# First-stage stores issued from GpSimd's queue, sums in a buffer of their own, longer transfer allowances in the planner

## The chip, the cores and the metric

The kernel runs on one core of a Trainium2 chip. The metric is device time in microseconds (us) of one execution. Five engines work side by side, each through its own instructions in a fixed order: TensorE (PE in the profile) multiplies, VectorE (DVE) and ScalarE (ACT) compute on tiles, GpSimd (POOL) and SyncE (SP) here issue transfers (DMAs). An instruction that has to wait holds back everything behind it on its engine, a transfer's issue included.

## The reference

Three steps, 4608 tokens (8 batches of 576), model width 512, inner width 2048:

```python
k_p = k.reshape(B, H, S // 8, 8, D).mean(axis=3)      # keys and values pooled by 8
v_p = v.reshape(B, H, S // 8, 8, D).mean(axis=3)
attn = softmax(q @ k_p.T / sqrt(D))                   # 8 heads of 64
x = (attn @ v_p) as [4608, 512]
x = square(relu(x @ w_in)) @ w_out                    # first feed-forward block
h = x @ w2_in
out = maximum(0.01 * h, h) @ w2_out                   # second feed-forward block
```

The four weight matrices arrive as 64-bit floats, which the kernel reads as pairs of 32-bit words and turns into 32-bit floats itself.

## The kernel before

**Stages.** The program has three stages one after the other. The first (about 0 to 604 us of the trace) computes attention and `h1 = square(relu(x @ w_in))`; the second (`Middle`) multiplies h1 by w_out; the third (`Second`) is the second feed-forward block. Each product is split into high and low parts, so a 512-column product takes three matmuls.

**The first stage.** Tokens go in 9 blocks of 512 (`blk`), inner columns in 16 groups of 128 (`c`). One pair (blk, c) is a *unit*: 12 matmuls of 512 columns into one PSUM bank (line 999), a relu out of the bank into a tile `r` or `st` (line 1010), a square in place (line 1013), and a store of 256 KB to `h1` in HBM (line 1029). The second stage multiplies by a scheme with sums, so for even blocks the sum of two neighbouring units' squares is stored too (addition at line 1035, store at line 1038). Tiles `r`, and `st` for odd units from block 2 on, have three buffers each; a relu waits until the buffer it is to write has been read by everyone, its store included.

**The order.** `START` and the first 16 units (`first_products`, `HAND = 16`) stand in an order written by hand; their stores go to GpSimd's queue. All that follows in the first stage is put in order by a planner: `FirstStage` lists operations with their engine, a cost in us, a rank, what they come after (`after`) and which buffers they take (`gets`) or touch (`uses`), and `Plan.run` always takes the operation that can start first by these figures. The figures only decide the order in which instructions stand on each engine; the chip then runs each engine's list in order, whatever the true durations are. A transfer counts as finished `lag` us after its issue. In the planned part the stores go to SyncE's queue, the same that loads keys, values, queries and words:

```python
def dma(self, fn, rank, kb, n=1, **k):
    return self.op("SP", 0.35 * n, fn, rank, lag=2.2 + kb / 180.0, **k)
```

**Attention's chain.** For each batch, keys and values are loaded (`add_keys`, `add_v`: 1 MB each, a key tail of 128 KB into `raw`, a value remainder of 384 KB in six transfers) and pooled on VectorE (the key tail at line 567). For each tile of 128 tokens, TensorE transposes q (line 681) and computes scores (line 727), ScalarE and VectorE make probabilities, TensorE transposes these (line 807, and line 815 for the last keys), ScalarE copies the high part out of the bank (line 821), VectorE the low part (line 824), and TensorE multiplies with the values (lines 868 to 871). All of these take PSUM banks from one set of four, `ps`.

**Words.** `add_stored` converts 38 half-tiles of the later weights within the first stage: load (line 345), exponent on ScalarE (line 243), bits and terms on VectorE (lines 247 to 264), sums (line 407), stores of 128 to 512 KB.

**Sums.** Before, the sum of an even block is added in place, into the first of the two squares' tiles, and the store of the sum reads that tile. The addition therefore has to wait until the store of that first square has read its tile.

Of the kernel before, what the change touches and what calls it, by code (L numbers as in the profile page):

```python
# [9 lines left out]
F32 = mybir.dt.float32  # L10
# [6 lines left out]
P = 128  # L17
# [26 lines left out]
def attention_relu2_leaky_kernel(  # L44
# [266 lines left out]
    class Weights:  # L311
# [5 lines left out]
        def load(self, n):  # L317
            self.steps[n][0]()
# [10 lines left out]
    class Stored:  # L329
# [10 lines left out]

        def load(self, h, tag="val"):
            w, kind, _, i, n = self.jobs[h]
            t = sb([P, 512, 2], U32, tag)
            for src, to in half_words_of(w, kind, i, n):
                nc.sync.dma_start(out=to(t), in_=src)
            return t[:, :, 0], t[:, :, 1]
# [674 lines left out]
    def store_parts(blk, c, r, queue):  # L1021

        t0 = blk * T
        n = T if blk else T // 2
        late = slice(t0 + T - n, t0 + T)
        s = {}

        def square_out():
            queue.dma_start(out=h1[c // 2, :, c % 2, t0 : t0 + T], in_=r())
            if c % 2 == 0:  # L1030
                evens[blk, c // 2] = r()

        def total():
            s[0] = evens[blk, c // 2][:, T - n :]
            nc.vector.tensor_tensor(out=s[0], in0=s[0], in1=r()[:, T - n :], op=ALU.add)

        def total_out():
            queue.dma_start(out=h1[c // 2, :, 2, late], in_=s[0])

        return [square_out] + ([total, total_out] if c % 2 and not blk % 2 else [])  # L1040
# [129 lines left out]
    class Plan:  # L1170

        SLACK = {"PE": 1.5, "ACT": 0.3, "DVE": 0.3, "SP": 0.3}

        def __init__(self, counts):
            self.ops, self.counts, self.rings, self.n = [], counts, {}, 0

        def op(self, engine, us, fn, rank, after=(), gets=(), uses=(), lag=0.0):
            x = Op(engine, us, fn, rank, lag)  # L1180
            for y in after:
                if y is not None:
                    y.then.append(x)
                    x.waits += 1
            x.gets = list(gets)
            for b in (*gets, *uses):
                b.users.append(x)
            x.order = len(self.ops)
            self.ops.append(x)
            return x  # L1190
# [16 lines left out]
        def run(self):  # L1207
# [3 lines left out]
            while left:  # L1211
# [17 lines left out]
                x.fn()  # L1229
                for y in x.then:  # L1230
                    y.ready = max(y.ready, x.end + x.lag + self.SLACK[y.engine])
                    y.waits -= 1
                    if not y.waits:
                        open_.append(y)
            self.now = now

    class FirstStage:
# [17 lines left out]
        def dma(self, fn, rank, kb, n=1, **k):  # L1255
            return self.op("SP", 0.35 * n, fn, rank, lag=2.2 + kb / 180.0, **k)

# [177 lines left out]
        def add_unit(self, blk, c, n):  # L1435
# [17 lines left out]
            x = self.plan.op("ACT", 0.63, lambda: square(at["r"]), 2, after=[x], uses=[r])  # L1453
            steps = store_parts(blk, c, lambda: at["r"], nc.sync)
            y = self.plan.op("SP", 0.35, steps[0], 0, after=[x], uses=[r], lag=3.0)
            if len(steps) > 1:
                x = self.plan.op("DVE", 0.69 if blk else 0.42, steps[1], self.SUMS,
                                 after=[x, self.even], uses=[r, self.even_r])
                self.plan.op("SP", 0.35, steps[2], 0, after=[x], uses=[self.even_r], lag=3.0)
            self.even, self.even_r = y, r  # L1460

        def add_stored(self, jobs):
            words, before = {}, None
            for h in jobs:
                _, kind, name, i, n = stored.jobs[h]
                val, gl = Buffer(f"wo{h % 2}"), Buffer("gl")
                R = self.STORED
                st = {}

                def run(fn, st=st):  # L1470
                    return lambda: fn(st)

                x = self.dma(run(lambda st, h=h: st.update(zip(("low", "top"), stored.load(h, f"wo{h % 2}")))),
                             R, 512, n=1 + kind, gets=[val], after=[self.units[2, 0]])
                x = self.op("ACT", 0.67, run(lambda st: exponent(st["top"])), R, after=[x], uses=[val])
# [43 lines left out]
        def run(self):  # L1519
# [26 lines left out]
            stored.at = STORED_EARLY  # L1546
            attention += self.last
            self.add_second_stage(attention)
            plan.run()

        def add_second_stage(self, attention):
            plan, last = self.plan, BLOCKS - 1
            opened_ = plan.op("SP", 0.0, middle.open, 0, after=attention)
            for four in (0, 1):
                for p in range(PAIRS):
                    if four:
                        after = [self.units[last, 2 * p + 1]]
                    else:
                        after = attention + [self.units[last - 1, FC - 1]]
                    x = plan.op("SP", 0.35, lambda four=four, p=p: middle.load_weights(four, p), 5,  # L1560
# [7 lines left out]
            for g in range(3):  # L1568
                x = plan.op("SP", 0.7, lambda g=g: middle.load(g), 5,
                            after=[opened_, self.units[last, 5 + g]], lag=5.0)  # L1570
                if g < 2:
                    steps = {}
# [12 lines left out]
    class Middle:  # L1585
# [16 lines left out]
        def open(self):  # L1602
            opened.pop().release()
            pool = tc.alloc_tile_pool(name="ms", bufs=1, side="left", reuse_waits="tile")
            opened.append(pool)
            nc.gpsimd.memset(pool.tile([P, 56], F32, tag="off", name="off"), 0.0)
            POOLS.update({f"m{n}{i}": pool for n in "hl" for i in range(3)})
# [80 lines left out]
        def group(self, g):  # L1688
            t0, n, r, four, p = self.at(g)
            steps = []  # L1690
            for x in range(g + 1, min(g + 5, self.GROUPS)):
                l, e = self.ahead(x)
                if x - l == g:
                    steps.append(lambda x=x: self.load(x))
            for x in range(g + 1, min(g + 3, self.GROUPS)):
                if x - self.ahead(x)[1] == g:
                    steps += self.prepare(x)
# [586 lines left out]
```

## Time and profile before

| | |
|---|---|
| median of three runs | 1687.83 us (1687.49 to 1690.32) |
| the profiled execution, its own time | 1688.77 us |
| its span, first to last instruction | 1687.0 us |
| TensorE busy | 1629.1 us (97% of the span) |
| VectorE busy | 1266.8 us (75%) |
| ScalarE busy | 835.6 us (50%) |
| mean TensorE clock that was granted | 0.992 of full speed |

So 1.77 us of the profiled execution lie outside the span. TensorE is busy nearly all the time; the profile's clock line falls below full speed only where TensorE has just stood. The second and third stages run from about 605 us to the end.

### The profile page before, as it was taken

Reading aid. Unit: us, or ns where it says so; the run is one execution under the profiler, and the core shown is the slowest. Engines: PE = TensorE matmul, PEld = TensorE weight load, DVE = VectorE, ACT = ScalarE, POOL = GpSimd, SP = SyncE. Lnnn points to the kernel's source line nnn. Section 1 sums busy time; section 2 is a strip of 40 time slices with the busy share of each in tenths; the row PEclk is TensorE's granted clock in tenths of the full one; section 3 lists DMA queues with packets and bytes.
Section 4 is the critical chain, followed back from the end, with each engine's and each line's share of the span. In section 5 each row is a group of like instructions: output and inputs, shape, how many; then the busy total and the mean of one; then the engine's idle time right before and its main releaser. Section 6 shows DMA issues by size and latency. Waiting matters only on the chain. (4 is left out here: it accounts for less than half of the span.)

```text
span 1687.0 us, 26627 instructions
## 1 busy us (share of the span) xinstructions
PE 1629.1 (97%) x9560; PEld 1472.9 (87%) x9560; DVE 1266.8 (75%) x2214; ACT 835.6 (50%) x1797; POOL 14.6 (1%) x30
## 2 busy tenths in 40 slices
PE   7897999989999979999999999999999999999998
PEld 6786887778888878888888899999999999999998
DVE  6885589878875488786869978878867876666665
ACT  6665676646765564434434554434444643333332
POOL 0110000000000000000000000000000000000000
PEclk9998999999999999999999999999999999999999
DMA  8726576768567977665758676476548754554443
GB/s 240 255 76 181 152 235 204 216 221 256 178 231 241 311 255 239 205 232 190 244 177 287 232 241 216 159 235 220 183 152 258 263 181 150 159 158 156 151 151 107
DMA packets 282756, 345.78 MB, mean 205 GB/s; under 512 B 55360, under 2 KB 201280, under 8 KB 282624
## 3 DMA queue, kind: packets, MB, share of 16 engines
q1 hardware_dynamic: 280480, 338.57, 62.0%
q0 software_dynamic: 1568, 4.98, 0.8%
q8 instruction: 75, 1.23, 0.3%
q10 hardware_dynamic: 576, 0.52, 0.1%
q14 instruction: 57, 0.47, 0.1%
HBM read 208.74 MB, written 135.27 MB: 204 GB/s over the span
## 5 line engine op out<-in xcount | busy, mean ns | idle before, releaser
L999 PE MATMUL acc<-xh,wi 128*128 128x512 f32 x640 | 224.9, 408 | 4.9 <-ACT r L1010 3.6
L999 PE MATMUL acc<-wo,wi 128*128 128x512 f32 x704 | 191.4, 399 | 8.8 <-ACT r L1010 8.8
L999 PEld LDWEIGHTS acc<-wo,wi 128*128 128x128 f32 x704 | 130.0, 189 | 35.0 <-ACT r L1010 9.6
L999 PEld LDWEIGHTS acc<-xh,wi 128*128 128x128 f32 x640 | 122.9, 192 | 30.7 <-ACT r L1010 4.6
L999 PE MATMUL acc<-xl,wi 128*128 128x512 f32 x320 | 127.1, 397 | 0.1
L2168 PE MATMUL ps<-wi,hh 128*128 128x256 f32 x512 | 93.9, 283 | 0.0
L2168 PE MATMUL acc<-wi,hh 128*128 128x256 f32 x496 | 91.1, 283 | 0.0
L2168 PE MATMUL ps<-wo,hh 128*128 128x256 f32 x496 | 90.9, 283 | 0.0
L1662 ACT CAST mh<-ms 128x512 fp32r<-128x512 f32 (+2 forms) x68 | 52.5, 771 | 76.7 <-DVE ms L1644 76.7
L2168 PE MATMUL acc<-wo,hh 128*128 128x256 f32 x484 | 88.8, 283 | 0.0
L1925 PE MATMUL acc<-fh,wo 128*128 128x384 f32 x384 | 83.0, 338 | 3.1 <-DVE gh L1938 2.0
L1010 ACT ACTIVATE r<-acc 128x512 f32<-128x512 f32 x88 | 53.2, 608 | 62.8 <-PE acc L999 38.5
L749 ACT ACTIVATE s<-ps,m 128x72 f32<-128x72 f32 x240 | 74.1, 334 | 19.3 <-DVE m L737 19.2
L1925 PE MATMUL ps<-fh,wi 128*128 128x384 f32 x384 | 82.3, 336 | 0.2 <-DVE gh L1938 0.2
L1941 ACT ACTIVATE gh<-gh 128x384 f32<-128x384 f32 x48 | 25.3, 527 | 112.3 <-DVE gh L1938 112.3
L2168 PEld LDWEIGHTS ps<-wi,hh 128*128 128x128 f32 x512 | 79.9, 192 | 0.0
L2168 PEld LDWEIGHTS acc<-wi,hh 128*128 128x128 f32 x496 | 77.4, 192 | 0.0
L2168 PEld LDWEIGHTS ps<-wo,hh 128*128 128x128 f32 x496 | 77.4, 192 | 0.0
L1707 PE MATMUL acc<-mh,wi 128*128 128x512 f32 (+1 forms) x256 | 77.2, 367 | 0.1
L1707 PE MATMUL ps<-mh,wi 128*128 128x512 f32 (+1 forms) x256 | 77.1, 367 | 0.0
L2168 PEld LDWEIGHTS acc<-wo,hh 128*128 128x128 f32 x484 | 75.5, 192 | 0.0
L2168 PE MATMUL ps<-wi,hl 128*128 128x256 f32 x256 | 72.4, 283 | 0.0
(350 smaller groups left out, 4365.9 us busy)
## 6 DMA issues: line engine op xcount, KB each, us to landing
h<-r SPq DMA_DIRECT2D x104, 256.0 KB
hf<-r SPq DMA_DIRECT2D x96, 192.0 KB
ml<-h SPq DMA_DIRECT2D x34, 512.0 KB
ml<-h SPq DMA_DIRECT2D x60, 256.0 KB
hr<-hf SPq DMA_DIRECT2D x23, 640.0 KB
xl<-hf SPq DMA_DIRECT2D x23, 640.0 KB
xh<-hf SPq DMA_DIRECT2D x23, 640.0 KB
h<-st SPq DMA_DIRECT2D x56, 256.0 KB
```

The source lines that it names most:

```text
L749: nc.scalar.activation(out=s[:, g, :], in_=at["ps"][:, h * SP : (h + 1) * SP], func=AF.Exp, bias=m[:, g : g + 1], accum_out=l[:, g : g + 1],)
L999: nc.tensor.matmul(acc_of[blk, c], lhsT=(wih, wil)[w][c][:, kc], rhs=xsplit[blk][x][kc], start=(kc, n) == order[0], stop=(kc, n) == order[-1],
L1010: nc.scalar.activation(out=r, in_=ps, func=AF.Relu)
L1662: nc.scalar.copy(hi[:, at], y)
L1707: nc.tensor.matmul(at[s][:, :n], lhsT=w[:, wx, b, s * P : (s + 1) * P], rhs=x[:, a], start=p == 0 and m == 0, stop=p == PAIRS - 1 and m == 2,)
L1925: nc.tensor.matmul(at, lhsT=w[:, FORMS[j], kc], rhs=x[j][:, kc], start=m == 0 and j not in (4, 6), stop=m == 5, skip_group_check=True,)
L1941: nc.scalar.activation(out=out_, in_=x, func=AF.Lrelu)
L2168: nc.tensor.matmul(at[:, s * TR : (s + 1) * TR], lhsT=x[:, a, s * P : (s + 1) * P], rhs=w[:, b], start=p == 0 and s == 0 and m == 0, stop= ...
```

## The change

Five edits, all of which act on the first stage and its end:

1. In the planned part, stores of squares and sums are issued from GpSimd's queue instead of SyncE's (the planner counts 1.0 us for an issue and 4.0 us until the transfer has landed; before 0.35 and 3.0).
2. The sum goes into a buffer of its own (`gh`, for block 0 `wo3`), so the addition no longer writes into a tile that is being stored.
3. The planner counts `5.0 + kb / 90` us for a transfer from SyncE's queue instead of `2.2 + kb / 180`: 6.4 us instead of 2.9 for the key tail of 128 KB, 16.4 instead of 7.9 for 1 MB.
4. Words are loaded two halves to a tile (the halves' loads stand right behind one another, `behind=`), and may start after unit (1, 12) instead of unit (2, 0).
5. At the end of the stage: weights of the second stage whose tiles the words don't use wait for attention only; the parts of group 2 of the second stage are prepared within the plan; a small GpSimd memset goes away.

```diff
         def square_out():
             queue.dma_start(out=h1[c // 2, :, c % 2, t0 : t0 + T], in_=r())
-            if c % 2 == 0:
+            if c % 2 == 0 and blk % 2 == 0:
                 evens[blk, c // 2] = r()
 
         def total():
-            s[0] = evens[blk, c // 2][:, T - n :]
-            nc.vector.tensor_tensor(out=s[0], in0=s[0], in1=r()[:, T - n :], op=ALU.add)
+            s[0] = sb([P, T], F32, "gh" if blk else "wo3")[:, :n]
+            even = evens.pop((blk, c // 2))
+            nc.vector.tensor_tensor(out=s[0], in0=even[:, T - n :], in1=r()[:, T - n :], op=ALU.add)
...
-        SLACK = {"PE": 1.5, "ACT": 0.3, "DVE": 0.3, "SP": 0.3}
+        SLACK = {"PE": 1.5, "ACT": 0.3, "DVE": 0.3, "SP": 0.3, "POOL": 0.3}
...
         def dma(self, fn, rank, kb, n=1, **k):
-            return self.op("SP", 0.35 * n, fn, rank, lag=2.2 + kb / 180.0, **k)
+            return self.op("SP", 0.35 * n, fn, rank, lag=5.0 + kb / 90.0, **k)
...
-            steps = store_parts(blk, c, lambda: at["r"], nc.sync)
-            y = self.plan.op("SP", 0.35, steps[0], 0, after=[x], uses=[r], lag=3.0)
+            steps = store_parts(blk, c, lambda: at["r"], nc.gpsimd)
+            y = self.plan.op("POOL", 1.0, steps[0], 0, after=[x], uses=[r], lag=4.0)
             if len(steps) > 1:
+                total = Buffer("gh" if blk else "wo3")
                 x = self.plan.op("DVE", 0.69 if blk else 0.42, steps[1], self.SUMS,
-                                 after=[x, self.even], uses=[r, self.even_r])
-                self.plan.op("SP", 0.35, steps[2], 0, after=[x], uses=[self.even_r], lag=3.0)
+                                 after=[x, self.even], gets=[total], uses=[r, self.even_r])
+                self.plan.op("POOL", 1.0, steps[2], 0, after=[x], uses=[total], lag=4.0)
...
+                first = x = self.dma(run(load), R, 512, n=1 + kind, gets=[val] if n == 0 else (),
+                             uses=[val], after=[self.units[1, 12]], behind=first if n else None)
...
-                        after = attention + [self.units[last - 1, FC - 1]]
+                        after = both if p in (0, 1, 3) else attention
+                        after = after + [self.units[last - 1, FC - 1]]
...
-                if g < 2:
+                if g < 3:
```

**Where it moves instructions.** First SyncE's list where the planned part begins; `wo` tiles receive keys, values and words, `raw` queries and key tails, and `h` is h1. Before:

```order
L193 DMA wo_1209<-in_v 32x1x512 x6
L1029 DMA h_77<-r 128x512
L183 DMA wo_1243<-in_v 128x4x512
L1029 DMA h_77<-r 128x512 x2
L176 DMA wo_1286<-in_k 128x4x512
L212 DMA raw<-in_q 128x8x64 x2
L163 DMA raw<-in_k 64x512
L1038 DMA h_77<-r 128x256
L1029 DMA h_77<-r 128x512 x2
L176 DMA wo_1384<-in_k 128x4x512
L1038 DMA h_77<-r 128x256
```

The same stretch of SyncE's list in the change:

```order
L193 DMA wo_1239<-in_v 32x1x512 x6
L183 DMA wo_1305<-in_v 128x4x512
L176 DMA wo_1365<-in_k 128x4x512
L212 DMA raw<-in_q 128x8x64 x2
L163 DMA raw<-in_k 64x512
L212 DMA raw<-in_q 64x8x64 x2
L212 DMA raw<-in_q 128x8x64
L183 DMA wo_1600<-in_v 128x4x512
L346 DMA wo_1623<-in_moe_w_out 128x2x256 x4
L346 DMA wo_1642<-in_moe_w_out 128x2x256 x4
```

The stores are gone from it, to GpSimd's list (144 of squares and 40 of sums there now, 16 and 6 before), and two runs of four word loads stand ahead of where they began before.

Next VectorE's list in the part written by hand, at the first sum, with the semaphores that each instruction waits for (`DMASW` counts transfers of GpSimd's queue). Before:

```order
L307 TENSOR_TENSOR wi_470<-wo_464,wi_470 128x1024 [waits Activation_49]
L1035 TENSOR_TENSOR r<-r 128x256 [waits DMASW0_49,Activation_49]
L737 TENSOR_REDUCE m<-acc_531 128x4 [waits PE_49]
L737 TENSOR_REDUCE m<-ps 128x4 [waits PE_49]
L261 TENSOR_SCALAR wi_126<-wo_516 128x1024 [waits DVE_49]
```

And in the change:

```order
L307 TENSOR_TENSOR wi_470<-wo_464,wi_470 128x1024 [waits Activation_49]
L1037 TENSOR_TENSOR wo_526<-r 128x256 [waits Activation_49]
L738 TENSOR_REDUCE m<-acc_532 128x4 [waits PE_49]
L738 TENSOR_REDUCE m<-ps 128x4 [waits PE_49]
L261 TENSOR_SCALAR wi_126<-wo_516 128x1024 [waits DVE_49]
```

The order is the same; the addition no longer waits for a store, and the two score maxima behind it are what ScalarE's exponentials need.

Last TensorE's list where block 1 ends and block 2 begins (from `acc_1733`'s last parts on before, `acc_1671`'s in the change; the units of block 2 read `xh` and `xl`). Before:

```order
L999 MATMUL acc_1733<-wo_821,wi_1099 128x512
L868 MATMUL ps<-pth,v_hi 128x384
L869 MATMUL ps<-pth,v_lo 128x384
L870 MATMUL ps<-ptl,v_hi 128x384
L871 MATMUL ps<-ptr,v_rem 128x384
L999 MATMUL acc_1733<-wo_821,wi_1099 128x512
L999 MATMUL acc_1733<-st,wi_1099 128x512
L999 MATMUL acc_1733<-wo_821,wi_1099 128x512
```

In the change:

```order
L1000 MATMUL acc_1671<-wo_824,wi_1105 128x512
L808 MATMUL ps<-cst,s 128x128 x4
L816 MATMUL ps<-cst,prem_84 96x128 x2
L550 MATMUL ps<-cst,gh 128x128 x4
L556 MATMUL ps<-cst,km 128x64
L869 MATMUL ps<-pth,v_hi 128x384
L870 MATMUL ps<-pth,v_lo 128x384
L871 MATMUL ps<-ptl,v_hi 128x384
L872 MATMUL ps<-ptr,v_rem 128x384
```

The last probability transposes now stand right ahead of the value products that need them, with only the last keys' and two key transposes between, and no part of a unit of block 1 is left to stand among the value products.

## Rows read from the trace of the kernel before

Times are in us unless marked ns.

**Rows 1.** The page: its head, and the first line of busy times.

```profile
span 1687.0 us, 26627 instructions
...
PE 1629.1 (97%) x9560; PEld 1472.9 (87%) x9560; DVE 1266.8 (75%) x2214; ACT 835.6 (50%) x1797; POOL 14.6 (1%) x30
```

**Rows 2.** Windows: length, busy by engine (instructions), then granted clock, DMA share, GB/s.

```profile
45.00:85.00 40.00, 33.71 (x184) 28.33 (x184) 32.84 (x50) 27.16 (x84) 6.07 (x10) 0.96 0.78 248
...
125.00:160.00 35.00, 26.22 (x132) 21.69 (x130) 14.21 (x33) 15.24 (x60) 0.00 (x0) 0.85 0.59 173
160.00:250.00 90.00, 88.70 (x489) 75.27 (x488) 64.93 (x163) 66.16 (x229) 0.00 (x0) 1.00 0.64 193
250.00:262.00 12.00, 8.32 (x38) 6.65 (x37) 9.23 (x22) 4.86 (x21) 0.00 (x0) 0.86 0.51 162
...
298.00:325.00 27.00, 24.40 (x133) 19.51 (x132) 23.66 (x54) 19.41 (x73) 0.00 (x0) 1.00 0.69 207
...
362.00:380.00 18.00, 12.85 (x60) 10.53 (x59) 13.06 (x28) 9.94 (x37) 0.00 (x0) 0.81 0.71 232
380.00:590.00 210.00, 210.00 (x1009) 174.83 (x1007) 147.14 (x322) 130.47 (x324) 0.29 (x2) 1.00 0.75 243
590.00:600.00 10.00, 6.36 (x21) 5.11 (x22) 5.30 (x8) 7.01 (x11) 0.00 (x0) 0.83 0.71 237
...
605.00:625.00 20.00, 15.13 (x112) 13.79 (x113) 17.52 (x34) 8.99 (x18) 0.00 (x0) 1.00 0.83 274
```

**Rows 3.** Timelines near 65 us: start, length, instruction, in brackets idle before and releaser.

```profile
65.47 0.43 DVE L1035 TENSOR_TENSOR r<-r 128x256 f32<-128x256 f32 x1 [2.94 <-DMA h<-r]
...
68.89 0.56 PE L681 MATMUL ps<-cst,raw 128*128 128x128 f32 x2 [3.47 <-ACT s L749]
```

**Rows 4.** Timelines of SyncE's queue, ScalarE and TensorE, 127 to 151 us.

```profile
127.09 4.23 SPq L193 DMA_DIRECT2D wo<-in_v  x6
...
132.32 0.38 SPq L183 DMA_DIRECT2D wo<-in_v  x1
132.81 1.63 SPq L1029 DMA_DIRECT2D h<-r  x2
...
144.14 0.60 ACT L1010 ACTIVATE r<-acc 128x512 f32<-128x512 f32 x1 [4.35 <-DMA h<-r]
...
150.50 0.60 ACT L1010 ACTIVATE r<-acc 128x512 f32<-128x512 f32 x1 [5.76 <-DMA h<-r]
...
144.79 0.80 PE L999 MATMUL acc<-wo,wi 128*128 128x512 f32 x1 [4.07 <-ACT r L1010]
```

**Rows 5.** Source lines 1029 and 1038: GpSimd's issues, and from issue to landing.

```profile
L1038 POOL DMA_DIRECT2D h<-r x6: 542/546/1049, 54.7 to 106.3; - x6
...
DMA to landing us min/median/max: 2.0/3.7/6.6
...
DMA to landing us min/median/max: 2.3/2.5/6.3
```

**Rows 6.** Timelines of SyncE's queue and VectorE: one key tail, issue and use.

```profile
242.51 0.53 SPq L163 DMA_DIRECT2D raw<-in_k  x1
...
252.42 1.00 DVE L567 TENSOR_REDUCE kp<-raw 64x64 f32<-64x512 f32 x1 [5.60 <-DMA raw<-in_k]
```

**Rows 7.** Waits of VectorE, 45 to 625 us: in total, times, longest.

```profile
DVE r L1035 <- DMA h<-r: 20.6, 9, 6.6
...
DVE kp L567 <- DMA raw<-in_k: 10.7, 2, 5.6
```

**Rows 8.** Timelines of VectorE and ScalarE at 365 and 593 us.

```profile
365.01 0.69 DVE L1035 TENSOR_TENSOR r<-r,st 128x512 f32<-128x512 f32 x1 [6.63 <-DMA h<-r]
...
592.99 0.60 ACT L1010 ACTIVATE r<-acc 128x512 f32<-128x512 f32 x1 [5.39 <-DMA h<-r]
```

**Rows 9.** Timeline of TensorE at 189 us; groups by form (count, busy, mean ns), 125 to 600 us.

```profile
189.22 0.49 PE L999 MATMUL acc<-xh,wi 128*128 128x512 f32 x1 [1.21 <-ACT xh L880]
...
L821 ACT CAST pth<-ps 128x512 fp32r<-128x512 f32 x28 | 16.6, 593 | 17.7 <-PE ps L807 17.3
...
L824 DVE TENSOR_TENSOR ptl<-ps,pth 128x512 fp32r<-128x512 f32 x28 | 19.3, 688 | 3.1 <-ACT pth L821 2.7
```

More of the change, by code (lines that the diff above doesn't have):

```diff
@@ L339, in begin, with load @@
             self.at = end
-        def load(self, h, tag="val"):
+        def load(self, h, t=None):
             w, kind, _, i, n = self.jobs[h]
-            t = sb([P, 512, 2], U32, tag)
+            if t is None:
+                t = sb([P, 512, 2], U32, "val")
             for src, to in half_words_of(w, kind, i, n):
@@ L1170, in attention_relu2_leaky_kernel, with op @@
     class Plan:
-        SLACK = {"PE": 1.5, "ACT": 0.3, "DVE": 0.3, "SP": 0.3}
+        SLACK = {"PE": 1.5, "ACT": 0.3, "DVE": 0.3, "SP": 0.3, "POOL": 0.3}
         def __init__(self, counts):
             self.ops, self.counts, self.rings, self.n = [], counts, {}, 0
-        def op(self, engine, us, fn, rank, after=(), gets=(), uses=(), lag=0.0):
+        def op(self, engine, us, fn, rank, after=(), gets=(), uses=(), lag=0.0, behind=None):
             x = Op(engine, us, fn, rank, lag)
@@ L1182, in op @@
                 if y is not None:
-                    y.then.append(x)
+                    y.then.append((x, True))
                     x.waits += 1
+            if behind is not None:
+                behind.then.append((x, False))
+                x.waits += 1
             x.gets = list(gets)
@@ L1229, in run @@
                 x.fn()
-                for y in x.then:
-                    y.ready = max(y.ready, x.end + x.lag + self.SLACK[y.engine])
+                for y, ends in x.then:
+                    if ends:
+                        y.ready = max(y.ready, x.end + x.lag + self.SLACK[y.engine])
                     y.waits -= 1
@@ L1465, in add_stored @@
                 _, kind, name, i, n = stored.jobs[h]
-                val, gl = Buffer(f"wo{h % 2}"), Buffer("gl")
+                if n == 0:
+                    val, tiles = Buffer(f"wo{i % 2}"), {}
+                gl = Buffer("gl")
                 R = self.STORED
@@ L1471, in run, with load @@
                     return lambda: fn(st)
-                x = self.dma(run(lambda st, h=h: st.update(zip(("low", "top"), stored.load(h, f"wo{h % 2}")))),
-                             R, 512, n=1 + kind, gets=[val], after=[self.units[2, 0]])
+                def load(st, h=h, i=i, n=n, tiles=tiles):
+                    if n == 0:
+                        tiles[0] = sb([P, 2, 512, 2], U32, f"wo{i % 2}")
+                    st["low"], st["top"] = stored.load(h, tiles[0][:, n])
+                first = x = self.dma(run(load), R, 512, n=1 + kind, gets=[val] if n == 0 else (),
+                             uses=[val], after=[self.units[1, 12]], behind=first if n else None)
                 x = self.op("ACT", 0.67, run(lambda st: exponent(st["top"])), R, after=[x], uses=[val])
@@ L1546, in run, with add_second_stage @@
             stored.at = STORED_EARLY
-            attention += self.last
-            self.add_second_stage(attention)
+            self.add_second_stage(attention, attention + self.last)
             plan.run()
-        def add_second_stage(self, attention):
+        def add_second_stage(self, attention, both):
             plan, last = self.plan, BLOCKS - 1
@@ L1605, in open @@
             opened.append(pool)
-            nc.gpsimd.memset(pool.tile([P, 56], F32, tag="off", name="off"), 0.0)
             POOLS.update({f"m{n}{i}": pool for n in "hl" for i in range(3)})
@@ L1694, in group @@
                     steps.append(lambda x=x: self.load(x))
-            for x in range(g + 1, min(g + 3, self.GROUPS)):
+            for x in range(max(g + 1, 3), min(g + 3, self.GROUPS)):
                 if x - self.ahead(x)[1] == g:
```

## Prediction

> **What bounds the kernel now.** I read the page's busy line first: TensorE works 1629.1 of 1687.0 us, VectorE three quarters of the time and ScalarE half [rows 1]. So nothing is gained by making another engine faster; time is gained only where TensorE stands, and the two later stages run without a gap worth naming. The windows come next, because they say where it stands: length less TensorE's busy time. That is 6.29 us in 45 to 85, 8.78 in 125 to 160, 1.30 in 160 to 250, 3.68 in 250 to 262, 2.60 in 298 to 325, 5.15 in 362 to 380, nothing in 380 to 590, 3.64 in 590 to 600 and 4.87 in 605 to 625 [rows 2]: 36 us. Five of these stretches also show a granted clock under full speed. One minus the clock, times the length, is 1.6, 5.25, 1.7, 3.4 and 1.7 us, 13.6 together. As TensorE stood for a part of that time, only a part of it was lost; I take half, with nothing and all as bounds.
>
> Then the timelines, for who ends the waits. In the part written by hand the first sum stands 2.94 us for a store, and TensorE then stands 3.47 us behind the exponentials whose maxima are queued behind that sum [rows 3]. At 125 to 160 two stores are issued behind six remainder loads (4.23 us of issuing) and a load of 1 MB; they are issued at 132.81, and the relu that needs the tile starts at 144.14, 11.3 us later, after 4.35 us of standing; another stands 5.76 us, and TensorE stands behind the relu [rows 4]. At 252 the key tail is used 9.9 us after its issue, VectorE having stood 5.60 us [rows 6]; the planner had counted 2.9. At 365 it is a sum again, 6.63 us, and at 593 a relu, 5.39 us [rows 8]. VectorE's waits say the same in total: 20.6 us for stores ahead of sums, 10.7 us for key tails [rows 7]. So every large stall is an engine standing in order at an instruction whose transfer came later than the planner thought.
>
> **The change part by part.** *Stores from GpSimd.* The same stores, issued by hand from GpSimd earlier on, cost 542 ns to issue (1049 at worst) and landed after 2.3 to 3.7 us in the median, 6.6 at worst [rows 5], in a stretch with more traffic (248 GB/s) than the 173 GB/s of 125 to 160, where SyncE's took 11.3 [rows 2, 4]. The planner now counts 1.0 + 4.0 us for them, which covers the median. 184 issues of 0.54 us are 100 us on an engine that is busy 14.6 [rows 1, 5], so issuing costs nothing; its cover is that GpSimd has no other work. If a sum is late, its store holds up the next unit's store and so a tile `r`, of which there are three. Recovered in full, 125 to 160 is worth 8.78 + 2.6 = 11.4 us, 362 to 380 5.15 + 1.7 = 6.9, and 590 to 600 3.64 + 0.85 = 4.5. With three tiles some waits for the unit before must remain, so I take 8.5, 5.0 and 3.5, about three quarters; bounds nothing and all.
>
> The Trainium skill, "DMA: Bandwidth & Descriptors", section "Issuing engines are not separate DMA queues", says that transfers of all issuers run on the same 16 DMA engines and interleave, and that another issuer saves only the issuing. By that the stores would land about as late as before; what it gives is the first rival. The rows on GpSimd's landing times speak against it here.
>
> The Trainium skill, "SBUF — State Buffer", section "🔬 SBUF: two separate sides", warns that VectorE in a two-port mode can keep GpSimd from writing a transfer's descriptors. The longest issue in the trace of before is 1.05 us beside a median of 0.54, so if that happened it was short; by the rule some stores would be issued later, but the sum above doesn't take it in.
>
> *A buffer for the sum.* The 2.94 us of wait in the hand part goes, with its likes, and with it most of 45 to 85: 6.29 + 0.8 = 7.1 at most; part of the idle time there is of other waits, so 5.5. The sums at 365 are in the term above.
>
> *Longer allowances.* The key tail counts 6.4 us now (6.7 with slack), against 9.9 measured [rows 6]. Of the 7 us by which it came late, 3.5 are now planned around. So of 250 to 262 (3.68 + 0.85 = 4.5) I take 2.5, and of 298 to 325 (2.60), where the other long key wait of [rows 7] lies, 2.2, since the stores no longer stand in front of the tail's queue either. Bounds nothing and all.
>
> *Words.* Two halves to a tile make runs of 1 MB, and two runs, 2 MB, can now stand ahead of a key or value load; at 248 GB/s [rows 2] that is 8.5 us. The values are needed many units later, so mostly it costs nothing; what hides it is the units' matmuls planned ahead, and only block 2's attention is just in time. There I charge the moved order: where it turns from block 1 to 2, the last probability transposes stand right ahead of their value products, and the copies between, 593 ns on ScalarE and 688 ns on VectorE (some 0.4 more for the last keys' part, worked out as its share of the columns), have only short transposes beneath, where TensorE idled 1.21 before [rows 9]. Between no loss and 2.5 us, I take 1. For other waits that a new order brings with it I take 3: the lower bound is the 210 us of the same planner without a gap, the upper two new stalls as at 250 to 262, 3.68 + 1.7 each, 11 us.
>
> *The end.* With group 2 prepared within the plan and weights loaded earlier, of 4.87 us in 605 to 625 [rows 2] I take half, 2.4; bounds nothing and all. The memset is one instruction on an idle engine: nothing.
>
> The sum: 5.5 + 8.5 + 2.5 + 2.2 + 5.0 + 3.5 + 2.4 = 29.6, less 4 is 25.6 us. From the profiled execution's own 1688.77 that is 1663.2; the median of the runs is 0.9 lower than that execution, so **1662 us**. All idle time and all clock back without a new cost would be 50 us, 1638; half of the terms with the whole of the costs is 14.8 − 13.5, nearly no gain.
>
> **The rivals.** *The queue doesn't matter.* If the same DMA engines make the stores land as late as before, the relus go on standing; left are 5.5 + 2.5 + 2.2 + 2.4, half of the 5.0 (the sum no longer waits, the relu does), less 4: 11.1 us, **1677**. For it: in 125 to 160 the stores stood behind bulk loads that will still run. Against it: [rows 5]. 0.12.
>
> *New waits eat the gain.* Word runs 8.5 us long ahead of a load that is just in time: two of them late by that much, in full on TensorE, cost 17 us, and with 5 of clock 22, which leaves 4: **1684**, and 1678 to 1690 around it. For it: attention of blocks 2 and later is fed by loads that stand behind words on one queue. Against it: the longer allowances make the planner start what depends on them later. 0.12, of which 0.04 still faster, 0.06 the same and 0.02 slower.
>
> *The sums' buffer becomes the stall, and the kernel slower.* From block 2 on 32 sums go to `gh`, which has two buffers and which the masked keys use too. If each sum has to wait until an earlier store has landed at the worst value seen, 6.6 us [rows 5], against 5.3 counted with slack, VectorE stands 1.3 us each; the maxima behind it are what ScalarE and then TensorE wait for. 32 by 1.3 is 42 us: **1704**. It decides from 25.6 / 32 = 0.8 us of TensorE's time for each sum. For it: in the hand part 2.94 us of one such wait reached TensorE as 3.47 [rows 3]. Against it: two buffers leave a unit pair's time, and later blocks have slack in VectorE. 0.08, of which 0.01 the same.
>
> **How the numbers follow.** The forecast gets 0.68, with a range of its own of 1648 to 1670: the low end is all of the 36 us of idle time and half of the clock's 13.6, less 3 of cost (40 us), the high end four fifths of the terms with 2 us more of costs (18 us). Over all cases 1648 to 1682 leaves out some 0.15: the slower rival, half of the second, a little below. A change of less than 0.2%, 3.4 us, is about what a measurement of this kernel can't tell from none. Faster: 0.68 + 0.12 + 0.04 = 0.84; the same: 0.06 + 0.01 = 0.07; slower: 0.02 + 0.07 = 0.09.
>
> **What would show it.** The step on the queue is right if GpSimd's list has some 190 issues of about 0.54 us, landing in 2 to 7 us, if ScalarE's waits for stores are gone and TensorE is busy through the stretch that answers to 125 to 160. The sum's buffer is right if VectorE's 20.6 us at line 1035 fall to nearly nothing. The allowances are right if the wait at the key tail is half of 10.7 or less. The cost at the turn to block 2 shows as TensorE waiting for ScalarE's or VectorE's copies of probabilities. Wrong would make it: stores from GpSimd landing after 10 us, a wait of VectorE for the sums' stores, or loads of keys and values standing behind words.

## The result, and the profile after

| | before | after |
|---|---|---|
| median of the runs beside each other | 1688.62 us | 1660.01 us (1658.12 to 1662.21, 4 runs) |
| ratio | | 0.983, 95% interval 0.9813 to 0.9847 |
| the profiled execution, its own time | 1688.77 us | 1660.31 us |
| span | 1687.0 us | 1658.5 us |

The change makes the kernel 1.7% faster, 28.6 us by the medians; 1662 was forecast. The page's busy line, against [rows 1]:

```profile
PE 1618.0 (98%) x9560; PEld 1470.8 (89%) x9560; DVE 1264.1 (76%) x2214; ACT 834.4 (50%) x1797; POOL 102.4 (6%) x191
```

TensorE's busy time fell by 11.1 us with the same 9560 matmuls, and its idle time (span less busy) from 57.9 to 40.5 us, by 17.4; together these are the 28.5 us of the span. The windows of the first stage show where it stood less, against [rows 2]; the stretches are moved where the program now gets there earlier. The columns are those of [rows 2].

```profile
45.00:85.00 40.00, 38.45 (x227) 32.67 (x226) 38.41 (x61) 31.05 (x106) 7.64 (x12) 1.00 0.81 263
...
125.00:160.00 35.00, 33.29 (x181) 28.06 (x180) 24.70 (x60) 21.24 (x77) 5.44 (x10) 1.00 0.65 194
...
160.00:200.00 40.00, 34.66 (x179) 28.41 (x178) 32.64 (x80) 26.98 (x105) 3.24 (x6) 0.91 0.74 225
...
240.00:252.00 12.00, 5.05 (x15) 4.20 (x16) 7.54 (x18) 5.68 (x22) 0.00 (x0) 0.60 0.64 185
...
298.00:325.00 27.00, 27.00 (x147) 22.81 (x146) 23.91 (x60) 21.81 (x88) 3.24 (x6) 1.00 0.75 214
...
362.00:380.00 18.00, 17.00 (x94) 13.71 (x93) 17.31 (x43) 13.35 (x56) 3.79 (x7) 1.00 0.80 235
```

Length less TensorE's busy time was 6.29 us at 45 to 85 and is 1.55; 8.78 at 125 to 160, now 1.71, with the clock at 1.00 in place of 0.85; 2.60 at 298 to 325, now nothing; 5.15 at 362 to 380, now 1.00. Two stretches became worse: 160 to 200 idles 5.34 us, and 240 to 252 idles 6.95 at a granted clock of 0.60. In the first, TensorE's longest stand is one of 2.7 us where block 1 turns into block 2, at 172.09: the key transposes (line 550) wait for the masked keys that VectorE writes at line 524. The timelines of SyncE's queue, VectorE and TensorE show the second:

```profile
235.82 1.02 SPq L410 DMA_DIRECT2D w1o<-wo  x1
...
244.16 0.43 DVE L408 TENSOR_TENSOR wo<-gl 128x256 f32<-128x256 f32 x1 [9.40 <-DMA w1o<-wo]
...
246.94 1.12 PE L682 MATMUL ps<-cst,raw 128*128 128x128 f32 x4 [7.92 <-DVE ptl L825]
```

Line 410 stores a part of a converted word from the tile that line 408 writes for the next word. The store was issued 8.3 us before VectorE got on, on the queue on which a run of four word loads had been issued just before (at 225.80), and TensorE stood 7.92 us. The waits over 45 to 625 us (in total, times, longest), against [rows 7], and then GpSimd's stores, against [rows 5]:

```profile
ACT r L1011 <- DMA h<-r: 6.7, 2, 3.9
...
DVE wo L408 <- DMA w1o<-wo: 16.4, 4, 9.4
...
PE ps L550 <- DVE gh L524: 2.7, 1, 2.7
```

The same kernel, the source line that issues the stores:

```profile
L1030 POOL DMA_DIRECT2D h<-r x88: 539/539/829, 47.1 to 585.1; - x88
...
DMA to landing us min/median/max: 2.3/4.2/7.1
```

VectorE's 20.6 us for stores at the sums and 10.7 us at the key tails are gone from its list, ScalarE's waits for stores are 6.7 us where they were 22.7, and GpSimd's stores of squares took 0.54 us each to issue and landed after 2.3 to 7.1 us. These are the signs that the prediction named, but for ScalarE's waits, which it wanted gone. But a kernel can show every sign and owe its time to something else, so the edits were taken apart.

The three stages in us, the first from the span's start, each to the first matmul of the next (in TensorE's timeline), the third to the end of its last matmul, all from the one profiled execution; the last column is the median of each kernel's own runs:

| kernel | first | second | third | median |
|---|---|---|---|---|
| before | 604.2 | 360.1 | 718.2 | 1688.62 |
| after | 584.1 | 351.0 | 718.8 | 1660.01 |
| b_queue | 599.6 | 365.0 | 718.2 | 1692.28 |
| b_sum | 588.4 | 360.4 | 720.5 | 1672.70 |
| b_sum_queue | 593.3 | 360.2 | 717.6 | 1676.74 |
| b_lag | 629.6 | 355.7 | 718.3 | 1711.80 |
| a_queue | 587.7 | 353.5 | 720.0 | 1667.12 |
| a_inplace | 593.8 | 355.3 | 718.8 | 1672.19 |
| a_lag | 594.7 | 351.9 | 718.7 | 1673.16 |
| a_words | 606.4 | 349.0 | 718.0 | 1678.34 |
| a_end | 584.7 | 360.5 | 719.3 | 1669.64 |
| a_words_out | 584.1 | 351.1 | 718.5 | 1663.03 |
| a_store8 | 607.9 | 348.7 | 718.9 | 1681.88 |
| a_store6_32 | 586.3 | 353.5 | 755.2 | 1699.82 |

So 20.1 us of the gain lie in the first stage and 9.1 in the second. TensorE's idle time in the first stage fell from 44.3 to 29.4 us; in the second from 5.5 to 2.7.

### The profile page after: what moved, and what is told of

Same layout as the page of the kernel before. It is cut to its first block, busy times and chain, and to the rows that moved or that the text cites. A ratio compares the mean times of both kernels' runs of the same rounds, so it can differ in the third digit from the quotient of the medians.

```text
span 1658.5 us, 26685 instructions
## 1 busy us (share of the span) xinstructions
PE 1618.0 (98%) x9560; PEld 1470.8 (89%) x9560; DVE 1264.1 (76%) x2214; ACT 834.4 (50%) x1797; POOL 102.4 (6%) x191
## 5 line engine op out<-in xcount | busy, mean ns | idle before, releaser
L1000 PE MATMUL acc<-xh,wi 128*128 128x512 f32 x640 | 221.3, 403 | 0.1
```

Source lines behind the costliest of these rows:

```text
L1000: nc.tensor.matmul(acc_of[blk, c], lhsT=(wih, wil)[w][c][:, kc], rhs=xsplit[blk][x][kc], start=(kc, n) == order[0], stop=(kc, n) == order[-1],
```

## The experiments

Names that begin with b_ are the kernel before with one part of the change (two in b_sum_queue); with a_, the changed kernel without one part, and in the last three with something more. Ratios are to runs of the kernel before on the same chip.

**The stores' queue, with the order on TensorE, VectorE and ScalarE kept.** The same edit in the one kernel and undone in the other:

```diff
-            steps = store_parts(blk, c, lambda: at["r"], nc.sync)     # b_queue
+            steps = store_parts(blk, c, lambda: at["r"], nc.gpsimd)   # undone in a_queue
```

> The kernel before with one edit: the planned part's stores are issued from GpSimd; the planner's figures, and with them the order on TensorE, VectorE and ScalarE, stay as before; sums still in place. If the queue is what made the stores late, the three terms of the prediction for it come back, 8.5 + 5.0 + 3.5 = 17 us (bounds 0 and 22.8): about 1671 us, ScalarE's 22.7 us of waits for stores gone, GpSimd's stores landing in 2 to 7 us. If the same DMA engines make them late whatever the queue: 1688 within 3 us, landings near 10 us. If the order had to change too: half of it, about 1679.

b_queue measured 1.0007 (0.9997 to 1.0016): nothing. Its waits over 45 to 625 us (in total, times, longest):

```profile
DVE r L1035 <- DMA h<-r: 28.7, 11, 9.8
DVE kp L567 <- DMA raw<-in_k: 15.7, 3, 7.8
...
DVE wo L407 <- DMA w1o<-wo: 9.2, 2, 8.7
...
DVE wo L485 <- DMA wo<-in_k: 6.0, 1, 6.0
...
ACT r L1010 <- DMA h<-r: 12.1, 6, 5.0
```

The same kernel, the source line that issues the stores:

```profile
DMA to landing us min/median/max: 2.3/3.9/8.3
```

And more of VectorE's waits over 45 to 625 us in the kernel before:

```profile
DVE r L1035 <- ACT st L1010: 9.6, 1, 9.6
...
DVE r L1035 <- ACT r L1010: 6.8, 1, 6.8
DVE wo L485 <- DMA wo<-in_k: 4.9, 1, 4.9
...
DVE wo L407 <- DMA w1o<-wo: 1.4, 1, 1.4
```

The stores do land early, 3.9 us in the median, 8.3 at worst, and ScalarE's waits for them fell from 22.7 to 12.1 us. In 125 to 160 TensorE idles 5.30 us in place of 8.78. VectorE's waits at the in-place sums fell too: those put down to stores are 28.7 us and were 20.6, but all its waits at line 1035, whatever they are put down to, fell from 45.7 to 39.0 us. (The two longest, 9.84 and 5.65 us near 575 and 583, stand where the kernel before stood 9.6 and 6.8, there put down to ScalarE.) The stands of 4.40 us at 140.85 and of 6.63 us at 365.01 for a store are gone. In their place VectorE waits longer for transfers of SyncE's queue, on which the stores no longer are. The key load that it pools at line 485 is waited for 6.0 us, and was 4.9; the two long waits for key tails take 7.78 and 7.34 us, and took 5.60 and 5.14; and at 367.75 VectorE stands 8.67 us for a store of a word, with TensorE 7.14 behind it. b_sum and b_sum_queue below, which also differ by the queue alone, show the same for the key tails: 5.59 and 5.18 us, and 7.40 and 7.23 with the stores on GpSimd's queue. Why these loads land later when the stores come from another queue, no run shows. In the profiled execution the first stage is 4.6 us shorter than before and the second 4.9 us longer. The 17 us of the expectation failed, and so did "landings near 10 us".

> The changed kernel with its stores issued from SyncE again, order of the other engines unchanged (the planner still counts GpSimd's figures); the loads now also stand behind stores in SyncE's list. If the queue is the cause: 17 us lost, about 1677, with ScalarE waiting for stores again in the stretch after 125 us. If the queue doesn't matter: 1660 within 3. If the order made with 5 us allowed for a store is what helps: a loss of under 8, about 1665.

a_queue measured 0.9866 (0.985 to 0.9883) where the change measured 0.983 (0.9813 to 0.9847): some 6 us lost, the third expectation's case (a loss of under 8). By the stages 3.6 us of it lie in the first; 2.5 lie in the second, where TensorE stands 4.42 us at 598.74 for ScalarE's parts of h1 (2.36 us in the change), and that this comes from the queue is not shown. One long wait is back, of ScalarE and behind it of TensorE:

```profile
ACT r L1011 <- DMA h<-r: 7.1, 1, 7.1
```

From the timelines of the same kernel:

```profile
141.34 0.80 PE L1000 MATMUL acc<-wo,wi 128*128 128x512 f32 x1 [4.97 <-ACT r L1011]
```

**The sums' own buffer.**

```diff
 def total():                                        # b_sum; the reverse in a_inplace
-    s[0] = evens[blk, c // 2][:, T - n :]
-    nc.vector.tensor_tensor(out=s[0], in0=s[0], in1=r()[:, T - n :], op=ALU.add)
+    s[0] = sb([P, T], F32, "gh" if blk else "wo3")[:, :n]
+    even = evens.pop((blk, c // 2))
+    nc.vector.tensor_tensor(out=s[0], in0=even[:, T - n :], in1=r()[:, T - n :], op=ALU.add)
```

> The kernel before with one edit: sums into their own buffer (the planner not told, its order kept, stores on SyncE in the planned part). By the prediction's term 5.5 us in the hand part, and half of the 5.0 at 362 to 380: 8 us, about 1680, VectorE's 20.6 us of waits for stores gone. By the rival on the sums' buffer: VectorE now waits for the store of an earlier sum, which SyncE's queue makes late: 1686 to 1695.

> The changed kernel with sums in place again, all else as it is. By the prediction's term 5.5 us of the hand part are lost and little else, as stores from GpSimd land in 4 us: about 1666, with the stall near 65 us back. If in-place sums cost in the planned part too, 10 us: 1670. If the hand part's stalls go for another reason: 1660 within 3.

b_sum measured 0.99 (0.9885 to 0.9915), 17 us faster and twice what was expected, with the stores still on SyncE's queue. a_inplace measured 0.9892 (0.9875 to 0.9908): 10 us are lost, as in its second expectation. Its waits, and then the stall of [rows 3], back in place:

```profile
DVE r L1036 <- DMA h<-r: 27.6, 12, 10.3
```

From the timelines of the same kernel:

```profile
69.03 0.44 PE L682 MATMUL ps<-cst,raw 128*128 128x128 f32 x2 [3.52 <-ACT s L750]
```

VectorE waits 27.6 us for stores that GpSimd issues: the buffer takes the wait away, the queue does not.

> The kernel before with sums in their own buffer and the planned stores from GpSimd, its order kept. The sum alone measured 1672.7, the queue alone no gain. If the queue only pays once the sum doesn't write into the stored tile (with sums in place a tile goes through two transfers one after the other, from either queue), it adds about the 6 us that the changed kernel lost without it: 1666. If the queue is worth its full term on its own: 1656. If it is worth nothing in this order: 1672.

With both, 0.9922 (0.9905 to 0.994), some 4 us slower than with the buffer alone, at the edge of what the two intervals tell apart; the first stage is 4.9 us longer. So in this order the queue adds nothing to the buffer, which is nearest to the third expectation (1672). What came to the end of the line there, in the timelines of SyncE's queue, VectorE and TensorE:

```profile
125.83 2.29 SPq L176 DMA_DIRECT2D wo<-in_k  x1
...
128.23 10.79 SPq L212 DMA_DIRECT2D raw<-in_q  x2
...
142.31 1.23 DVE L485 TENSOR_TENSOR wo<-wo 128x1024 f32<-128x1024 f32 x1 [8.25 <-DMA wo<-in_k]
...
143.73 0.47 PE L868 MATMUL ps<-pth,v_hi 128*128 128x128 f32 x1 [7.30 <-DVE kt L563]
```

A key load of 1 MB was issued at 125.83 and its pooling (line 485) started at 142.31, 16.5 us later; the old order counts 7.9 us for it, so VectorE stands 8.25 us there and TensorE 7.30. With stores on the same queue (b_sum) the same load took 12.3 us:

```profile
127.63 0.38 SPq L176 DMA_DIRECT2D wo<-in_k  x1
...
139.97 1.22 DVE L485 TENSOR_TENSOR wo<-wo 128x1024 f32<-128x1024 f32 x1 [6.34 <-DMA wo<-in_k]
```

So in 125 to 160 two things were late in the kernel before, the stores and the key load, for which VectorE stood 4.9 us there too (the row of line 485 above). The stores' queue only takes the first away, and the second is what the allowances are for: the new one for 1 MB is 16.4 us.

**The allowances.**

```diff
-            return self.op("SP", 0.35 * n, fn, rank, lag=2.2 + kb / 180.0, **k)   # a_lag
+            return self.op("SP", 0.35 * n, fn, rank, lag=5.0 + kb / 90.0, **k)    # b_lag
```

> The changed kernel with the old allowances for SyncE's transfers, 2.2 + kb / 180. By the prediction's terms 2.5 + 2.2 us are lost, the waits at the key tails (10.7 us on VectorE) come back: about 1665. If the allowances cost as much as they save, because they made the order in which the store of words near 236 us comes late (VectorE waits 9.40 us there): 1660 within 3, or down to 1652 if that wait goes and no other comes.

> The kernel before with one edit, the new allowances. By the same terms 4.7 us: about 1685, key-tail waits gone, waits for stores as before. If longer allowances move bulk loads ahead of the stores on SyncE's queue: no gain or a loss, 1688 to 1700.

a_lag measured 0.9902 (0.9885 to 0.9919), 12 us lost and not 4.7. VectorE's waits there, and then two of TensorE's:

```profile
DVE kp L568 <- DMA raw<-in_k: 9.8, 1, 9.8
DVE gl L247 <- DMA w1o<-gl: 8.8, 1, 8.8
...
DVE wo L486 <- DMA wo<-in_k: 7.2, 1, 7.2
```

From the timelines of the same kernel:

```profile
295.20 0.66 PE L816 MATMUL ps<-cst,prem 128*96 128x128 f32 x2 [6.54 <-DVE ptl L825]
...
366.62 0.45 PE L816 MATMUL ps<-cst,prem 128*96 128x128 f32 x1 [8.06 <-DVE ptl L825]
```

Key tail and key load are waited for again. Behind the key tail TensorE stands 6.54 us, where the change idles nothing in 298 to 325, and behind the key load 5.94 us, at 139.99. The 8.06 us, where the change idles 1.00 us in 362 to 380, are behind neither: VectorE stands 8.84 us at line 247 there for a store of a word, so a part of the loss is of the order and not of loads. b_lag, the same edit alone, measured 1.013 (1.0114 to 1.0146), 22 us slower and beyond both expectations. Its trace shows two things: VectorE waits at the in-place sums as long as before (45.7 us by all causes, with the key-tail waits gone), and the end of the stage has a new stall.

```profile
DVE r L1035 <- DMA h<-r: 43.1, 13, 9.7
```

From the timelines of the same kernel:

```profile
615.60 1.51 SPq L1674 DMA_DIRECT2D wo<-w1o  x3
...
629.64 0.58 PE L1707 MATMUL ps<-mh,wo 128*128 128x256 f32 x1 [33.73 <-ACT mh L1662]
```

Longer allowances make the planner put the words later, until the last of them stand at the very end of the stage. In the kernel before, eight of the second stage's weight loads (line 1674, into `wo`) wait for the last word; here the first three are issued at 615.60, the eighth at 619.5, where before all eight went out between 569.8 and 576.7, and TensorE stands 33.73 us.

**The words, and the end of the stage.** a_words undoes edit 4 and a_end edit 5 of the change, whole:

```diff
-                first = x = self.dma(run(load), R, 512, n=1 + kind, gets=[val] if n == 0 else (),
-                             uses=[val], after=[self.units[1, 12]], behind=first if n else None)
+                x = self.dma(run(lambda st, h=h: st.update(zip(("low", "top"), stored.load(h, f"wo{h % 2}")))),
+                             R, 512, n=1 + kind, gets=[val], after=[self.units[2, 0]])    # a_words
...
-            self.add_second_stage(attention, attention + self.last)                                      # a_end
+            attention += self.last
+            self.add_second_stage(attention, attention)
...
-                if g < 3:
+                if g < 2:
...
+            nc.gpsimd.memset(pool.tile([P, 56], F32, tag="off", name="off"), 0.0)
...
-            for x in range(max(g + 1, 3), min(g + 3, self.GROUPS)):
+            for x in range(g + 1, min(g + 3, self.GROUPS)):
```

> The changed kernel with the words as before: one half to a tile, loads from unit (2, 0) on. The prediction gave this edit nothing but the moved order's waits (4 us), so by it 1656 to 1660, and the wait near 244 behind word loads gone or moved. The kernel before with the new allowances alone stood 33.73 us at the end of the stage, for weights that wait for the last words; if it is this edit that cures that, the stall is back: 1680 to 1695. If the edit at the end cures it, it isn't.

> The changed kernel with the end of the stage as before (all weights of the second stage wait for words, group 2 outside the plan, the memset). By the prediction's term 2.4 us are lost: about 1662. If this edit is what cures the 33.73 us stall that the allowances make at the end: 1680 to 1695. If neither this nor the words' edit alone is needed (each cures it): 1662 here and under 1662 without the words' edit.

a_words measured 0.9933 (0.9918 to 0.9948), 17 us lost; in its trace:

```profile
601.62 0.98 SPq L1679 DMA_DIRECT2D wo<-w1o  x2
...
606.36 0.58 PE L1712 MATMUL ps<-mh,wo 128*128 128x256 f32 x1 [28.88 <-ACT wo L1685]
```

So it is the words' edit that pays for the allowances: loads in pairs and from unit (1, 12) on bring the last word in before the stage ends (which of the two does it, no run separates). In this edit the prediction had seen only a cost. a_end measured 0.9879 (0.9863 to 0.9895), 8 us lost, but its first stage is as long as the change's, 584.7 against 584.1: all of it is in the second stage, whose 360.5 us are those of the kernel before (360.1). Groups of matmuls by form, 625 to 935 us (count, busy, mean ns), of the change and then of a_end:

```profile
L1720 PE MATMUL acc<-mh,wi 128*128 128x512 f32 x192 | 63.0, 389 | 0.0
...
L1720 PE MATMUL acc<-wo,wi 128*128 128x512 f32 x80 | 22.2, 389 | 0.0
...
L1720 PE MATMUL acc<-xl,wi 128*128 128x512 f32 x24 | 9.3, 389 | 0.0
```

```profile
L1722 PE MATMUL acc<-mh,wi 128*128 128x512 f32 x192 | 64.4, 396 | 0.0
...
L1722 PE MATMUL acc<-wo,wi 128*128 128x512 f32 x67 | 17.8, 389 | 0.0
...
L1722 PE MATMUL acc<-xl,wi 128*128 128x512 f32 x21 | 8.2, 392 | 0.0
```

The same matmul takes 396 ns with its moving operand in a tile `mh` and 389 with it in `wo` in a_end, and 389 with either in the change. Tiles `mh` and `ml` lie in the pool in which the memset's tile `off`, 56 floats for each partition, stood ahead of them. But `xl`, which lies in another pool that `off` doesn't move, is slower in a_end too, by less: 392 ns against 389.

**Stores of words, from another queue or with more time.**

```diff
-            nc.sync.dma_start(out=to[:, 5:7], in_=o[:, :, 0])       # and the four others of Stored: a_words_out
+            nc.gpsimd.dma_start(out=to[:, 5:7], in_=o[:, :, 0])
...
-                            uses=[gl, sums, *more], lag=3.5)
+                            uses=[gl, sums, *more], lag=8.0)        # a_store8; 6.0 in a_store6_32
-    STORED_EARLY = 38
+    STORED_EARLY = 32                                               # a_store6_32 alone
```

> The changed kernel with the stores of converted words issued from GpSimd too, order of the other engines unchanged. VectorE's 9.40 us of wait at 244 for such a store, issued from SyncE at 235.82 behind word loads, should go, and with it TensorE's 7.92 us and the low clock (0.60 over 12 us, 4.8 us at most) after it: 8 to 12 us, 1648 to 1652. If those stores stand in front of the squares' stores in GpSimd's list and wait for VectorE there, ScalarE waits for tiles and it gives nothing: 1660 to 1668. If it is transfers that take long and not the place in SyncE's list, 1660 within 3.

a_words_out measured 0.9851 (0.9826 to 0.9875), no gain over the change. Timelines of VectorE and TensorE:

```profile
235.52 0.42 DVE L408 TENSOR_TENSOR wo<-gl 128x256 f32<-128x256 f32 x1 [4.27 <-DMA w1o<-wo]
...
239.77 1.01 DVE L568 TENSOR_REDUCE kp<-raw 64x64 f32<-64x512 f32 x1 [3.17 <-DMA raw<-in_k]
...
241.55 0.69 PE L682 MATMUL ps<-cst,raw 128*128 128x128 f32 x2 [6.05 <-DVE ptl L825]
```

The wait at line 408 fell from 9.40 to 4.27 us, and the key tail, behind the same word loads, came late by 3.17 instead: TensorE still stands 6.05. Here too VectorE's list has the instruction earlier than its transfer lands.

> The changed kernel with one figure changed: the planner counts 8.0 us instead of 3.5 for the last store of each converted word (8.3 us measured from issue to the wait's end near 244). If VectorE's sums of the next words stand too early because of that figure, the 7.92 us of TensorE at 246.94 and the low clock there go, 8 to 12 us: about 1650. If the later words push the end of the stage, as in the kernel before with new allowances, it is lost there: 1660 or more. If the wait is replaced by that for the key tail (its issue stands behind the same word loads): a gain of 0 to 3.

a_store8 measured 0.9954 (0.9937 to 0.9971). Its window where the change stands (columns as in [rows 2]), and then the end of its first stage:

```profile
240.00:252.00 12.00, 12.00 (x68) 10.07 (x67) 9.15 (x23) 9.06 (x35) 3.19 (x7) 1.00 1.01 294
```

From the timelines of the same kernel:

```profile
607.89 0.58 PE L1720 MATMUL ps<-mh,wo 128*128 128x256 f32 x1 [36.02 <-ACT wo L1693]
```

TensorE is busy all through 240 to 252, so the store's 3.5 us were the cause of that stall; but the words moved later, as in b_lag, and 36.02 us were lost for the weights at the end, the second expectation's case.

> The changed kernel with two figures changed: 6.0 us counted instead of 3.5 for the last store of each converted word, and 32 instead of 38 half-tiles of words converted in the first stage; the other six follow in the third stage, among those that were there already. With 8.0 and 38 the stall at 246.94 went (TensorE's excess in 225 to 275 fell from 12.9 to 3.2 us), and 36.02 us were lost at the end of the stage for weights whose tiles the last words held until 603. If the two can be had apart, by having fewer words in the stage: 7 to 10 us less than the changed kernel in the same rounds' terms, 1650 to 1654. If 6.0 is too little for the stall or the order brings another: 1658 to 1663. If six more half-tiles on VectorE disturb the third stage, or the end of the first stage still waits: 1665 or more.

a_store6_32 measured 1.0066 (1.0054 to 1.0078), the last expectation's case. The first stage ends at 586.3; the third is 36 us longer. Timelines of TensorE and ScalarE:

```profile
365.17 1.09 PE L728 MATMUL ps<-kt,qt 128*128 128x144 f32 x3 [7.87 <-DVE ptl L825]
...
1261.67 0.69 PE L1938 MATMUL ps<-fh,wo 128*128 128x384 f32 x1 [27.94 <-ACT gh L1958]
...
1259.87 0.65 ACT L243 ACTIVATE val<-val 128x512 f32<-128x512 f32 x1 [7.16 <-DMA val<-in_moe_w_out]
```

In the third stage four half-tiles were left over; they were then loaded and converted one after the other, the first load 5.5 and each of the others 7.2 us of ScalarE's standing, and TensorE stood 27.94 us. In the first, another word's store made a stall at 365. No version faster than the change was found.

## Why the prediction was right, point by point

**What bounds it.** Right: all the stages' time that moved is TensorE's standing, the clock behind it, and (not seen) its pace in the second stage. That the two later stages had no gap worth naming was wrong of the second. The forecast of 1662 comes so near because errors of both signs offset each other, which is luck: the end of the stage and the second were to give 2.4 us, with the second untouched but for its start, and the second gave 9.1; the first stage was to give 23.2 (the other terms less 4) and gave 20.1.

**Stores from GpSimd, 17 us.** The step failed as a term of its own. Its premises held (0.54 us to issue, landing in 2 to 7 us), but alone the queue is worth nothing over the whole kernel, in the change some 6 us, 3.6 of them in the first stage. It was wrong to ask of the stall at 125 to 160 only which wait ended last: behind the store stood a key load that was nearly as late. At 365, priced at 5.0, a store of a word stood behind the sum: TensorE stands 7.14 us there in b_queue and 5.70 in b_sum, so neither edit recovers it by itself. The rival "the queue doesn't matter" came true for the kernel before, though not by its mechanism: the stores landed earlier, and waits for the loads, and for a word's store, took their place. The Trainium skill, "DMA: Bandwidth & Descriptors", section "Issuing engines are not separate DMA queues", holds that another issuer saves only the time of issuing; b_queue's time agrees, its landings (8.3 us at worst where [rows 4] has 11.3 for one) don't.

**The sums' buffer, 5.5 us.** Mis-sized: 17 us alone, 10 in the change. In-place sums waited for stores 9 times between 45 and 625 us [rows 7], and such a wait also holds back the relu that needs the tile; I had booked those stalls under the queue. The view of line 1038, the sums' stores of the kernel before, has who waited for them:

```profile
ACT r L1010: 14.3, 4
```

So 14.3 of ScalarE's 22.7 us were for sums' stores and not for squares', the 5.76 us at 150.50 [rows 4] and the 5.39 at 592.99 [rows 8] among them. The rival in which this buffer becomes the stall did not occur: no wait at line 1037 for a sum's store is among VectorE's in the change. In b_sum, with these stores on SyncE's queue, there are two such waits, 4.4 us.

**The allowances, 4.7 us.** Right in kind, too small, and not separable: 12 us in the change (a word's store included), 22 us slower alone. I priced the key tail of 128 KB alone and left out the key load of 1 MB, which took 12.3 and 16.5 us against 7.9 counted.

**The words, nothing but a cost.** Wrong: without this edit the allowances lose 29 us at the end of the stage (28.88 in a_words). The cost that I feared is there as well: 4 us were taken for the moved order, and 240 to 252 alone idles 6.95 us, with at most 4.8 more in the clock ((1 - 0.60) by 12 us); without this edit, in a_words, it idles 2.86 us at a clock of 1.00. At the turn to block 2, priced at 1 us, TensorE waits 2.7 us, for masked keys and not for the copies of probabilities that the prediction named.

**The memset, "one instruction on an idle engine: nothing".** Wrong in the step from the instruction to the edit: the edit also takes away the tile that it filled. From start to start, 512-column matmuls of the second stage take 232.4 ns in the mean in all six traces that have the tile (before, the four b_ kernels, a_end) and 227.7 in all eight without it; 4.7 ns by 1343 of them is 6.3 of the 9.1 us. That the tile and not another part of edit 5 does it is argued, from `wo`, whose pace is the same in both, and not shown by a run: the tile wasn't taken away alone, and the 3 ns more of `xl`, which it doesn't move, speak against its place as the whole cause. The rest, 2.8 us, is what TensorE's idle time fell by in the second stage, and fits the term of 2.4.

## What to carry to other kernels

When a stall has two transfers late side by side, taking away the one that ended last buys only what lies between the two: look at what the engine would wait for next, before booking the whole stall to one edit. When one kind of transfer gets another queue, check whether those left on the first land later, as the key tails did here. Edits to an order made by figures don't add up; each allowance that is lengthened pushes something else later, and the end of the stage has to be checked for what it pushed. An in-place update of a tile that is being stored makes two transfers follow each other; here a buffer cured that (b_sum, a_inplace), and another queue didn't.

## What the runs showed of the hardware

In the kernels with the tile `off`, a matmul of 512 columns ran 7 ns longer (396 against 389) for moving operands in tiles of the pool that it heads, some 3 ns longer for those in `xl`, and by 2 ns at most for those in `wo`; why is not shown. An issue on SyncE's queue can take long by itself: two query loads (the row at 128.23) behind 2.4 MB of key and value loads took 10.79 us to issue in b_sum_queue, the second of them 10.24, while GpSimd's issues in that kernel stayed at 0.54 us in the median and 1.05 at worst. The key tails landed later, by some 2 us, when the stores beside them came from GpSimd's queue (5.59 and 5.18 us of wait in b_sum, 7.40 and 7.23 in b_sum_queue). The Trainium skill, "SBUF — State Buffer", section "🔬 SBUF: two separate sides", lets one expect that VectorE can hold up a transfer issued by GpSimd; the longest of the change's 184 issues took 1.05 us, so no issue shows a long hold-up.
